# Half of the tiles of a matmul round moved to an idle PSUM pool, and an uneven split of the last output tile, in a fused attention + SwiGLU kernel

## The chip, the cores and the metric

The kernel runs on one core of a Trainium2 chip. The metric is the device time of one execution in microseconds (us), each figure a median of several runs. Every profile shown is from one execution, with times counted from the start of its span. Every timed run compared here is fast (granted TensorE clock 0.99 to 1.00).

Words used below: TensorE does the matmuls, VectorE and ScalarE move results from PSUM (the matmuls' accumulator memory, eight banks) to SBUF (the working memory), GpSimd issues most loads. To evacuate a bank is to move its result out, so that the next tile can have it. A load's issue is the row of the engine that starts it; it lands when its data is there.

## The reference

Attention through 32 memory slots per head, then a SwiGLU block, cut to what matters (8 batches, 8 heads, 576 positions, width 512, hidden width 1536):

```
a    = softmax(phi, over positions)              # per batch and head
k_m  = a^T k ;  v_m = a^T v                      # 32 x 64 memories
x    = softmax(q k_m^T / 8) v_m                  # tokens x 512
out  = (silu(x w_gate) * (x w_val)) w_out
```

The kernel folds `v_m` into the weights: U = v_m w, per batch, for gate and value. A "U round" below is the group of matmuls that makes U for one batch and one third ("chunk", 512 columns) of the hidden width; U is then multiplied with the attention weights to give gate and value.

## The kernel before

Two PSUM pools share the eight banks: `ps` (six) serves everything except output tiles, `po` (two) serves output tiles and, at the start, warm-up matmuls.

```python
work = ctx.enter_context(tc.tile_pool(name="work", bufs=3))
ps = ctx.enter_context(tc.tile_pool(name="ps", bufs=6, space=bass.MemoryType.PSUM))
po = ctx.enter_context(tc.tile_pool(name="po", bufs=2, space=bass.MemoryType.PSUM))
```

A U round fills two tiles for the gate weights and two for the value weights, then ScalarE ("a") and VectorE ("v") evacuate them:

```python
def u_round(b, parts, evac):
    banks = []
    for which, c, halves in parts:
        ...
        p = [ps.tile([128, 2, HC], FP32, tag="b", ...) for g in range(NG)]
        ...                      # matmuls into p[g]: rhs=W[w, c][64 * g:64 * g + 64, h0:h1, i]
        for g in range(NG):
            ...
            banks.append((dst, src, rSs[b][:, g, 0] if b in scaled else None))
    for (t, p, r), e in zip(banks, evac):
        ...                      # "a": nc.scalar.activation, "v": nc.vector.tensor_scalar
```

A slot makes one gate tile (ScalarE applies SiLU) and then the value tile of the slot before (VectorE multiplies it with that gate). So at each U round one value is left over:

```python
def gv_slot(b, s):
    n = len(pend)
    gv_gate(b, s)                # 2 matmuls into a ps bank, SiLU on ScalarE
    flush_mul(n)                 # 2 matmuls into a ps bank, multiplication on VectorE
```

The stretch of batches 0 and 1, and the last output tile:

```python
run([u_half(1, (0, 1), 0, 1, "av")] + g0[4:8] + g1[4:5])
for c in range(1, NCH):
    s = 8 * c
    run([u_item(0, c)] + g1[s - 3:s] + g0[s:s + 5])
    run([u_item(1, c)] + g0[s + 5:s + 8] + g1[s:s + 5])
run(g1[-3:])
flush_mul()
backlog = out_list(0) + out_list(1)
...
def out_units_end(c, u):         # two halves of 256 columns, each 12 matmuls,
    ...                          # a copy on ScalarE and two stores (SyncE and ScalarE queues)
```

Loads on GpSimd's queue (queries of batches 2 and 3 share one buffer):

```python
load_q(2)
load_q(3)                        # before the stretch; waits until batch 2's queries are transposed
...
if b == 2:                       # after the scores of batch 2
    load_k(3); load_v(3); load_q(4); load_phi(4, nc.gpsimd)
```

The softmax here doesn't subtract the row's maximum and nothing guards it: scores larger than these inputs give would overflow.

Of the kernel before, what the change touches and what calls it, by code (L numbers as in the profile page):

```python
# [9 lines left out]
FP32 = mybir.dt.float32  # L10
# [4 lines left out]
def kernel(  # L15
# [23 lines left out]
    DM, DF = moe_w_gate.shape  # L39
# [3 lines left out]
    NJF = DF // 128  # L43
# [11 lines left out]
# [3 lines that stand above are left out]
# [3 lines left out]
    out_r = out.rearrange("(b p j) c -> b j p c", b=B, p=P, j=J)  # L61
# [53 lines left out]
    HC = CH // 2  # L115
# [14 lines left out]
    WO = {}  # L130
# [234 lines left out]

    scaled = set()

    def u_round(b, parts, evac):


        banks = []
        for which, c, halves in parts:
            w0, w1, h0, h1 = which[0], which[-1] + 1, halves[0], halves[-1] + 1
            n = (h1 - h0) * HC
            p = [
                ps.tile([128, 2, HC], FP32, tag="b", name=f"p_u{g}").rearrange("p a f -> p (a f)")
                for g in range(NG)
            ]
            for w in which:
                o = (w - w0) * n  # L380
                for i in range(NP):
                    for g in range(NG):
                        nc.tensor.matmul(  # L383
                            p[g][32 * i:32 * i + 32, o:o + n],
                            lhsT=kTs[b][64 * g:64 * g + 64, 2, 32 * i:32 * i + 32],
                            rhs=W[w, c][64 * g:64 * g + 64, h0:h1, i],
                            start=True,
                            stop=True,
                            tile_position=(64 * g, 32 * i),
                        )  # L390
            for g in range(NG):
                if (b, c, g) not in Us:
                    Us[b, c, g] = upool.tile([128, 2, 2, HC], BF16, tag=f"U{c}{g}", name="t_U")
                if len(which) == 1:
                    dst = Us[b, c, g][:, h0:h1, w0]
                else:
                    dst = Us[b, c, g][:, h0]
                src = p[g][:, 0:(w1 - w0) * n].rearrange("p (a f) -> p a f", f=HC)
                banks.append((dst, src, rSs[b][:, g, 0] if b in scaled else None))
        for (t, p, r), e in zip(banks, evac):  # L400
            if e == "a":
                if r is None:
                    nc.scalar.copy(out=t, in_=p)  # L403
                else:
                    nc.scalar.activation(out=t, in_=p, func=AF.Copy, scale=r)
            elif r is None:
                nc.vector.tensor_copy(out=t, in_=p)  # L407
            else:
                nc.vector.tensor_scalar(out=t, in0=p, scalar1=r, scalar2=None, op0=ALU.mult)
# [5 lines left out]
    def flush_mul(n=None):  # L415
        for _ in range(len(pend) if n is None else n):
            pend.pop(0)()
# [16 lines left out]
    def gv_gate(b, s):  # L434

        jf, r = s // 2, s % 2
        if b % 2 == 0 and r == 0:
            hts[b // 2, jf] = hpool.tile([128, 2 * S], BF16, tag=f"h{jf}", name="t_h")
        gate = gv_half(b, s, 0)
        sg = work.tile([128, HALF], BF16, tag="sg", bufs=8, name="t_sg")  # L440
        nc.scalar.activation(out=sg, in_=gate, func=AF.Silu)  # L441
        col = (b % 2) * S + r * HALF
        dst = hts[b // 2, jf][:, col:col + HALF]

        def mul():
            val = gv_half(b, s, 1)
            nc.vector.tensor_tensor(out=dst, in0=sg, in1=val, op=ALU.mult)  # L447

        pend.append(mul)
# [14 lines left out]
    def token_segments(t0, count):  # L464
        segs = []
        t = t0
        while t < t0 + count:
            bb, rest = divmod(t, S)
            blk, pp = divmod(rest, P)
            n = min(P - pp, t0 + count - t)  # L470
            segs.append((t - t0, n, bb, 2 * (blk % 3) + blk // 3, pp))
            t += n
        return segs
# [30 lines left out]

    def out_units_end(c, u):

        h = DM // 2
        mine = {}

        def unit(half, jf):  # L510
            def run():
                if jf == 0:
                    mine["p"] = po.tile([128, h], FP32, tag="o", name="p_oo")
                nc.tensor.matmul(  # L514
                    mine["p"],
                    lhsT=hts[c, jf][:, 128 * u:128 * (u + 1)],
                    rhs=WO[jf][:, h * half:h * (half + 1)],
                    start=(jf == 0),
                    stop=(jf == NJF - 1),
                )  # L520
                if jf == NJF - 1:
                    t_o = work.tile([128, h], FP32, tag="to", name="t_o")
                    nc.scalar.copy(out=t_o, in_=mine["p"])
                    segs = token_segments(2 * c * S + 128 * u, 128)
                    for n, (r0, m, bb, jj, pp) in enumerate(segs):
                        (nc.sync, nc.scalar)[n % 2].dma_start(
                            out=out_r[bb, jj, pp:pp + m, h * half:h * (half + 1)],
                            in_=t_o[r0:r0 + m, :],
                        )

            return run

        return [unit(half, jf) for half in range(2) for jf in range(NJF)]

    def out_list(b):
        tiles = range(0, 4) if b % 2 == 0 else range(4, 9)
        res = []
        for n, u in enumerate(tiles):
            if b + 1 == B and u == tiles[-1]:
                res += out_units_end(b // 2, u)  # L540
            else:
                res += out_units(b // 2, u, "v" if n % 4 != 3 else "a")
        return res
# [3 lines left out]
            lambda g=g, n=n: q_T(b, g, n, evac[2 * g + n]) for g in range(NG) for n in range(2)  # L547
        ]

    def u_item(b, c, evac="avav"):  # L550

        return lambda: u_round(b, (((0,), c, (0, 1)), ((1,), c, (0, 1))), evac)

    def u_half(b, which, c, half, evac):

        return lambda: u_round(b, ((which, c, (half,)),), evac)

    def u_three(b):

        u_round(b, (((0,), 0, (0, 1)), ((1,), 0, (0, 1)), ((0,), 1, (0, 1))), "avavav")  # L560
# [4 lines left out]
    def run(items):  # L565
        for x in items:
            x()
# [13 lines left out]
    def gv_slots(b):  # L581
        return [lambda s=s: gv_slot(b, s) for s in range(2 * NJF)]
# [78 lines left out]

    g0, g1 = gv_slots(0), gv_slots(1)
    run([u_half(0, (0,), 0, 0, "av"), u_half(1, (0,), 0, 0, "av")])
    warm(6)
    for s in range(4):
        gv_gate(0, s)
    run([u_half(0, (1,), 0, 0, "va"), u_half(1, (1,), 0, 0, "va")])
    for s in range(2):
        gv_gate(1, s)
    flush_mul(3)  # L670
    run([u_half(0, (0, 1), 0, 1, "va")])
    flush_mul(2)
    run(g1[2:4])
    run([u_half(1, (0, 1), 0, 1, "av")] + g0[4:8] + g1[4:5])
    for c in range(1, NCH):
        s = 8 * c
        run([u_item(0, c)] + g1[s - 3:s] + g0[s:s + 5])
        run([u_item(1, c)] + g0[s + 5:s + 8] + g1[s:s + 5])
    run(g1[-3:])
    flush_mul()  # L680
    backlog = out_list(0) + out_list(1)
# [7 lines left out]
    for b in range(2, B):  # L689
# [30 lines left out]
        g = gv_slots(b)  # L720
# [3 lines left out]
        if last:  # L724
            streams += [([u_item(b, 2)], 5, 6)]
# [55 lines left out]
```

## Time and profile before

| | before |
|---|---|
| median time | 249.45 us (249.39 to 249.80, 3 runs) |
| TensorE busy | 96% of the span |
| first U round starts / first output matmul starts | 26.99 / 56.88 us |
| period of one U round with eight slots | 4.88 us |
| last output tile's first matmul / end of the span | 241.11 / 247.6 us |

The lines themselves stand in the prediction. In every row of a timeline the first number is the start and the second the duration. A pair of matmuls has a row of 0.41 us but the next pair starts 0.245 us later, so rows overlap, and stalls are read from the starts.

### The profile page before, as it was taken

The numbers are of one execution on the slowest core, as the hardware profiler recorded it, in microseconds if no ns is written. First come the engines' busy times: TensorE is split into PE (matmuls) and PEld (weight loads), VectorE is DVE, ScalarE is ACT, GpSimd is POOL, SyncE is SP. The second block draws the span as 40 slices with busy tenths as digits, with TensorE's granted clock in tenths as the row PEclk, the third lists the DMA queues.
The fourth block names the chain that finished last, engine by engine and source line by source line (L and its number), as shares of the span: only waits on it lengthen the run. The fifth ranks groups of instructions, "written<-read, shape, count | busy, mean of one in ns | idle before, by whom it ended". The sixth has DMA issues, their size and how long they took to land.

```text
span 247.6 us, 6587 instructions
## 1 busy us (share of the span) xinstructions
PE 237.5 (96%) x2573; PEld 152.3 (61%) x2600; DVE 158.9 (64%) x337; ACT 165.2 (67%) x356; POOL 54.5 (22%) x85
## 2 busy tenths in 40 slices
PE   7999999999999999999999999999999999999993
PEld 7966666665544765467645666476546655467543
DVE  0046599994437788479846778478846877587420
ACT  2447888886077667966896577966896577676201
POOL 8423455000060004060405420090007000000000
PEclk9999999999999999999999999999999999999998
DMA  7999999999689976996996599289425311310143
GB/s 182 206 204 203 196 197 201 233 199 198 134 158 248 231 168 95 207 282 145 125 243 191 94 175 249 91 119 196 94 51 123 65 42 42 87 42 0 45 128 85
DMA packets 49167, 37.00 MB, mean 149 GB/s; under 512 B 15984, under 2 KB 43888, under 8 KB 49136
## 3 DMA queue, kind: packets, MB, share of 16 engines
q0 software_dynamic: 27632, 22.42, 57.0%
q1 hardware_dynamic: 20496, 13.37, 22.7%
q10 hardware_dynamic: 1008, 0.79, 1.2%
q8 instruction: 20, 0.33, 0.5%
q14 instruction: 11, 0.09, 0.1%
HBM read 42.47 MB, written 9.44 MB: 210 GB/s over the span
## 4 chain that ended last, share of the span: by engine, by line
PE 87%; DMA 8%; POOL 2%; issue 2%; ACT 0%; POOLq 0%
PE p_oo L483 36%; PE p_g L425 20%; PE p_v L425 19%; DMA t_kv<-in_v_dram 8%; PE p_u L383 6%; PE p_kv L183 2%; PE p_oo L514 1%; POOL t_q L93 1%; POOL t_kv L81 1%; PE p_g L351 1%; PE p_v L351 1%; PE p_g L331 1%; PE p_vT L290 0%; PE p_kv L203 0%; PE p_oo L588 0%
## 5 line engine op out<-in xcount | busy, mean ns | idle before, releaser
L483 PE MATMUL p_oo<-WO,t_h 128*128 128x512 bf16 x393 | 101.6, 379 | 3.0 <-issue 2.9
L441 ACT ACTIVATE t_sg<-p_g 128x288 bf16<-128x288 f32 x192 | 76.9, 413 | 31.6 <-PE p_g L425 24.2
L447 DVE TENSOR_TENSOR t_h<-t_sg,p_v 128x288 bf16<-128x288 bf16 x192 | 84.3, 453 | 18.9 <-PE p_v L425 14.8
L425 PEld LDWEIGHTS <-t_U 128*128 128x128 bf16 x768 | 74.3, 98 | 30.7 <-issue 2.3
L425 PE MATMUL p_g<-t_A,t_U 128*128 128x288 bf16 x384 | 77.5, 286 | 0.4
L425 PE MATMUL p_v<-t_A,t_U 128*128 128x288 bf16 x384 | 76.8, 286 | 0.0
L483 PEld LDWEIGHTS <-t_h 128*128 128x128 bf16 x420 | 39.6, 98 | 41.0 <-issue 6.0
L495 DVE COPY t_o<-p_oo 128x512 f32<-128x512 f32 x27 | 18.6, 690 | 31.4 <-PE p_oo L483 31.3
L407 DVE CAST t_U<-p_u 128x512 bf16<-128x512 f32 x42 | 26.7, 684 | 6.8 <-PE p_u L383 6.8
L403 ACT CAST t_U<-p_u 128x512 bf16<-128x512 f32 x30 | 15.8, 592 | 8.9 <-PE p_u L383 8.9
L493 ACT COPY t_o<-p_oo 128x512 f32<-128x512 f32 x8 | 4.7, 589 | 19.9 <-PE p_oo L483 10.6
L100 POOL DMA_DIRECT2D t_q<-in_q_dram x6 | 4.7, 782 | 59.3 <-DMA t_qT<-t_q 58.5
L588 PE MATMUL p_oo<-bones 128*128 128x128 bf16 x198 | 15.7, 244 | 1.5 <-DVE bones L603 1.5
L383 PE MATMUL p_u<-W,t_kT 64*32 64x512 bf16 (+1 forms) x416 | 15.7, 365 | 0.1
L153 ACT ACTIVATE t_ephi<-t_phi 96x768 bf16<-96x768 f32 x16 | 12.5, 843 | 4.1 <-DMA t_phi<-in_phi_dram 4.1
L588 PEld LDWEIGHTS <-bones 128*128 128x128 bf16 x198 | 13.9, 111 | 2.1 <-DVE bones L603 1.5
L166 POOL COPY t_mark<-t_A 1x1 bf16<-1x1 bf16 x4 | 0.7, 181 | 55.7 <-DVE t_A L360 55.7
L341 ACT ACTIVATE t_E<-p_g 128x288 bf16<-128x288 f32 x16 | 6.6, 412 | 8.5 <-PE p_v L331 7.9
L360 DVE TENSOR_TENSOR t_A<-t_E,t_lz 128x576 bf16<-128x576 bf16 x16 | 11.5, 750 | 0.5 <-ACT t_lz L355 0.5
L355 ACT ACTIVATE t_lz<-t_lz 128x576 f32<-128x576 f32 x16 | 10.9, 684 | 0.5
L170 POOL TENSOR_TENSOR t_es<-t_es,t_ephi 96x256 f32<-96x256 f32 x16 | 10.7, 669 | 1.3
L383 PEld LDWEIGHTS <-t_kT 64*32 64x32 bf16 x416 | 4.8, 89 | 8.8 <-issue 7.3
(58 smaller groups left out, 167.9 us busy)
## 6 DMA issues: line engine op xcount, KB each, us to landing
t_kv<-in_k_dram POOLq DMA_DIRECT2D x8, 576.0 KB, 9.3
t_kv<-in_v_dram POOLq DMA_DIRECT2D x8, 576.0 KB, 14.2
out_dram<-t_o SPq DMA_DIRECT2D x23, 192.0 KB, 2.5
t_phi<-in_phi_dram POOLq DMA_DIRECT2D x6, 576.0 KB, 15.3
t_q<-in_q_dram POOLq DMA_DIRECT2D x6, 576.0 KB, 7.4
out_dram<-t_o SPq DMA_DIRECT2D x24, 128.0 KB, 2.5
W<-in_moe_w_gate_dram POOLq DMA_DIRECT2D x6, 256.0 KB, 12.9
W<-in_moe_w_val_dram POOLq DMA_DIRECT2D x6, 256.0 KB, 11.9
```

The lines of the kernel that those rows point to most:

```text
L153: nc.scalar.activation(out=t[:, :, g].rearrange("p j i m -> p i j m"), in_=src[:, g], func=AF.Exp)
L355: nc.scalar.activation(out=lz, in_=lz, func=AF.Exp, scale=-1.0)
L360: nc.vector.tensor_tensor(out=a, in0=es.pop((b, g)), in1=lzs.pop((b, g)), op=ALU.mult)
L383: nc.tensor.matmul(p[g][32 * i:32 * i + 32, o:o + n], lhsT=kTs[b][64 * g:64 * g + 64, 2, 32 * i:32 * i + 32], rhs=W[w, c][64 * g:64 * g + ...
L403: nc.scalar.copy(out=t, in_=p)
L407: nc.vector.tensor_copy(out=t, in_=p)
L425: nc.tensor.matmul(p[:, 0:HALF], lhsT=Us[b, c, g][:, o // 2, which, 128 * (o % 2):128 * (o % 2 + 1)], rhs=atts[b, g][:, r], start=(g == 0) ...
L441: nc.scalar.activation(out=sg, in_=gate, func=AF.Silu)
L447: nc.vector.tensor_tensor(out=dst, in0=sg, in1=val, op=ALU.mult)
L483: nc.tensor.matmul(mine["p"], lhsT=hts[c, jf][:, 128 * u:128 * (u + 1)], rhs=WO[jf], start=(jf == 0), stop=(jf == NJF - 1),)
L495: nc.vector.tensor_copy(out=t_o, in_=mine["p"])
L588: nc.tensor.matmul(p[:, 0:128], lhsT=bones, rhs=bones, start=True, stop=True)
```

## The change

The intent: while batches 0 and 1 are worked on, the two banks of `po` lie idle, so half of a U round's tiles (its value weights; in chunk 0 the whole of three half rounds) go there, and TensorE no longer waits for banks. At the end, an uneven split makes the last copy and the last store smaller.

```diff
-    def u_round(b, parts, evac):
+    def u_round(b, parts, evac, spare=-1):
-        for which, c, halves in parts:
+        for n_part, (which, c, halves) in enumerate(parts):
+            pool, tag = (po, "o") if n_part == spare else (ps, "b")
             p = [
-                ps.tile([128, 2, HC], FP32, tag="b", ...)
+                pool.tile([128, 2, HC], FP32, tag=tag, ...)
...
     def out_units_end(c, u):
-        h = DM // 2
+        parts = ((0, 3 * DM // 4), (3 * DM // 4, DM))
...
-    run([u_half(0, (1,), 0, 0, "va"), u_half(1, (1,), 0, 0, "va")])
+    run([u_half(0, (1,), 0, 0, "va"), u_half(1, (1,), 0, 0, "va", 0)])
...      # likewise the other half rounds of chunk 0
-        run([u_item(0, c)] + g1[s - 3:s] + g0[s:s + 5])
-        run([u_item(1, c)] + g0[s + 5:s + 8] + g1[s:s + 5])
+        run([u_item(0, c, spare=1)] + g1[s - 3:s] + g0[s:s + 5])
+        run([u_item(1, c, spare=1)] + g0[s + 5:s + 8] + g1[s:s + 5])
```

More of the change, by code (lines that the diff above doesn't have):

```diff
@@ L375, in u_round @@
             p = [
-                ps.tile([128, 2, HC], FP32, tag="b", name=f"p_u{g}").rearrange("p a f -> p (a f)")
+                pool.tile([128, 2, HC], FP32, tag=tag, name=f"p_u{g}").rearrange(
+                    "p a f -> p (a f)"
+                )
                 for g in range(NG)
@@ L505, in out_units_end, with unit @@
     def out_units_end(c, u):
-        h = DM // 2
+        parts = ((0, 3 * DM // 4), (3 * DM // 4, DM))
         mine = {}
-        def unit(half, jf):
+        def unit(c0, c1, jf):
             def run():
                 if jf == 0:
-                    mine["p"] = po.tile([128, h], FP32, tag="o", name="p_oo")
+                    mine["p"] = po.tile([128, c1 - c0], FP32, tag="o", name="p_oo")
                 nc.tensor.matmul(
@@ L516, in run @@
                     lhsT=hts[c, jf][:, 128 * u:128 * (u + 1)],
-                    rhs=WO[jf][:, h * half:h * (half + 1)],
+                    rhs=WO[jf][:, c0:c1],
                     start=(jf == 0),
@@ L521, in run @@
                 if jf == NJF - 1:
-                    t_o = work.tile([128, h], FP32, tag="to", name="t_o")
+                    t_o = work.tile([128, c1 - c0], FP32, tag="to", name="t_o")
                     nc.scalar.copy(out=t_o, in_=mine["p"])
@@ L526, in run @@
                         (nc.sync, nc.scalar)[n % 2].dma_start(
-                            out=out_r[bb, jj, pp:pp + m, h * half:h * (half + 1)],
+                            out=out_r[bb, jj, pp:pp + m, c0:c1],
                             in_=t_o[r0:r0 + m, :],
@@ L531, in unit @@
             return run
-        return [unit(half, jf) for half in range(2) for jf in range(NJF)]
+        return [unit(c0, c1, jf) for c0, c1 in parts for jf in range(NJF)]
     def out_list(b):
@@ L548, in q_items, with u_item, u_half @@
         ]
-    def u_item(b, c, evac="avav"):
-        return lambda: u_round(b, (((0,), c, (0, 1)), ((1,), c, (0, 1))), evac)
-    def u_half(b, which, c, half, evac):
-        return lambda: u_round(b, ((which, c, (half,)),), evac)
+    def u_item(b, c, evac="avav", spare=-1):
+        return lambda: u_round(b, (((0,), c, (0, 1)), ((1,), c, (0, 1))), evac, spare)
+    def u_half(b, which, c, half, evac, spare=-1):
+        return lambda: u_round(b, ((which, c, (half,)),), evac, spare)
     def u_three(b):
@@ L670 @@
     flush_mul(3)
-    run([u_half(0, (0, 1), 0, 1, "va")])
+    run([u_half(0, (0, 1), 0, 1, "va", 0)])
     flush_mul(2)
     run(g1[2:4])
-    run([u_half(1, (0, 1), 0, 1, "av")] + g0[4:8] + g1[4:5])
+    run([u_half(1, (0, 1), 0, 1, "av", 0)] + g0[4:8] + g1[4:5])
     for c in range(1, NCH):
         s = 8 * c
-        run([u_item(0, c)] + g1[s - 3:s] + g0[s:s + 5])
-        run([u_item(1, c)] + g0[s + 5:s + 8] + g1[s:s + 5])
+        run([u_item(0, c, spare=1)] + g1[s - 3:s] + g0[s:s + 5])
+        run([u_item(1, c, spare=1)] + g0[s + 5:s + 8] + g1[s:s + 5])
     run(g1[-3:])
```

## The prediction

> **What bounds the kernel now.** I read the page first (engine totals, slices, chain of waits), then the timeline of the stretch that the change touches, 26 to 57 us, engine by engine, then the timeline of the last 8 us.
>
> ```profile
> PE 237.5 (96%) x2573; PEld 152.3 (61%) x2600; DVE 158.9 (64%) x337; ACT 165.2 (67%) x356; POOL 54.5 (22%) x85
> PE 87%; DMA 8%; POOL 2%; issue 2%; ACT 0%; POOLq 0%
> ```
>
> The engine totals and the chain say the same: TensorE is the bound from 25.8 us to the end; the DMA share is the wait for the values of batch 1 before that. VectorE and ScalarE appear as no limit over the whole span. But "busy" hides short stalls, because a matmul's row is longer than the distance to the next one. So I read starts, not busy shares. In the stretch that the change touches, one round for U and eight gate/value slots repeat every 4.88 us (U rounds start at 40.62, 45.50, 50.38). One such period, TensorE only:
>
> ```profile
> 45.50 0.63 PE L383 MATMUL p_u<-W,t_kT 64*32 64x512 bf16 x16
> 46.06 0.42 PE L425 MATMUL p_g<-t_A,t_U 128*128 128x288 bf16 x2
> 46.32 0.41 PE L425 MATMUL p_v<-t_A,t_U 128*128 128x288 bf16 x2
> 46.72 0.41 PE L425 MATMUL p_g<-t_A,t_U 128*128 128x288 bf16 x2
> 46.96 0.41 PE L425 MATMUL p_v<-t_A,t_U 128*128 128x288 bf16 x2
> 47.29 0.41 PE L425 MATMUL p_g<-t_A,t_U 128*128 128x288 bf16 x2
> 47.59 0.41 PE L425 MATMUL p_v<-t_A,t_U 128*128 128x288 bf16 x2
> 47.84 0.41 PE L425 MATMUL p_g<-t_A,t_U 128*128 128x288 bf16 x2
> ```
>
> The columns are start, duration, engine, line and what is done. Undisturbed, two matmuls of 288 columns start every 0.245 us (47.59 to 47.84). Here the third pair comes 0.40 after the second (0.155 late), the fifth 0.33 after the fourth (0.085 late), the sixth 0.30 later (0.055 late). These add to 0.30 us per period, and the rest of the period has none. The evacuations that they wait for:
>
> ```profile
> 45.98 0.69 ACT L405 ACTIVATE t_U<-p_u,t_rS 128x512 bf16<-128x512 f32 x1 [0.20 <-PE p_u L383]
> 46.56 0.68 ACT L405 ACTIVATE t_U<-p_u,t_rS 128x512 bf16<-128x512 f32 x1
> 46.05 0.75 DVE L409 TENSOR_SCALAR t_U<-p_u,t_rS 128x512 bf16<-128x512 f32 x1
> 46.71 0.74 DVE L409 TENSOR_SCALAR t_U<-p_u,t_rS 128x512 bf16<-128x512 f32 x1
> 47.37 0.45 DVE L447 TENSOR_TENSOR t_h<-t_sg,p_v 128x288 bf16<-128x288 bf16 x1
> ```
>
> The pool has six banks and hands them out in turn. A U round takes four, the first gate and value the other two, and the next four tiles take over the four U banks. ScalarE's two evacuations end at 46.67 and 47.24, and the late gate pairs start 0.05 after each (46.72, 47.29). VectorE's second ends at 47.45 and the late value pair starts 0.14 later (47.59). So the waits are for banks, and I take 0.05 and 0.14 us as the delays from an end on ScalarE and VectorE to TensorE.
>
> **What the Trainium skill says.** "PSUM — Partial Sum Buffer", section "Specifications (TRN2)": 8 banks of 2 KiB. So the pools of six and two use all there is; the trace shows the pool of two used only by the 128x128 warm-up matmuls before the first output tile at 56.88. "Perfetto Trace Analysis", section "Optimization Strategy", says that a consistent bubble on the engine that should be saturated can mean too few buffers; the repeating late starts above are that. "TensorE: Matmul & The Clock Gate", section "Back-to-back issue gap", has N/2.4 + 2.5 ns for an isolated matmul, and says that loading weights makes it about 81 ns at N=128. The trace has 109.6 ns at 256 columns with changing weights (242.20 to 242.31 for one), which fits the first; for 128 columns it has the 24 warm-up matmuls in 1.51 us with a tail of 0.22, so 56 ns, though with the same weights reloaded. "Perfetto Trace Analysis", section "DMA Instruction — HWDGE (DVE, Sync)", says that the issuing sequencer is free for the next instruction only at the end of its DMA row. The trace agrees on ScalarE at the start (the issue at 0.74 takes 0.43, the table load begins at 1.2).
>
> **Part one: two of a U round's four tiles in the other pool.** No instruction is added or removed, the order on every engine stays (the comparison of instructions shows only line numbers moved). Per period U now holds two of the six banks and both of the other two; those two were last evacuated a period ago, so they never block. Then, from the start T of a U round:
> - Undisturbed starts on TensorE: gate 0 at 0.56, the leftover value at 0.81, gate 1 at 1.05, value 0 at 1.30, gate 2 at 1.54, value 1 at 1.79, gate 3 at 2.03, value 2 at 2.28.
> - In turn over six banks, gate 2 and value 1 take the two U banks: free at 1.22 and 1.44. No wait left. All three stalls of today go.
> - But value 2 now gets the bank of the leftover value (as today). VectorE multiplies that one only after both its U evacuations, from T+1.87 (47.37 - 45.50) for 0.45, plus 0.14: 2.46. Against 2.28 to 2.29 undisturbed that is a new wait of 0.17.
>
> So 0.30 becomes 0.17: 0.13 us per period, for the three periods from 40.62: 0.39 us. VectorE doesn't take over as the long-run bound: with work queued, its multiplications start 0.363 apart (47.37, 47.73) and its U evacuations 0.66 apart, 8 x 0.363 + 2 x 0.66 = 4.22 per period against 0.56 + 8 x 0.49 = 4.48 on TensorE.
>
> The first such period, from 35.75, is different:
>
> ```profile
> 35.75 0.89 PE L383 MATMUL p_u<-W,t_kT 64*32 64x512 bf16 x16
> 36.57 0.42 PE L425 MATMUL p_g<-t_A,t_U 128*128 128x288 bf16 x2
> 33.80 0.74 DVE L409 TENSOR_SCALAR t_U<-p_u,t_rS 128x512 bf16<-128x512 f32 x1
> 34.46 1.92 DVE L447 TENSOR_TENSOR t_h<-t_sg,p_v 128x288 bf16<-128x288 bf16 x5
> 36.30 0.74 DVE L409 TENSOR_SCALAR t_U<-p_u,t_rS 128x512 bf16<-128x512 f32 x1
> ```
>
> Here the gate follows U after 0.82 instead of 0.56: the second half of U itself waits for banks (0.26). With the other pool it does not. VectorE though is back to back from 30.58 to here (1.92 for five is 0.367 apart), so it reaches the leftover value no sooner than 36.30 + 2 x 0.66 = 37.62, and value 2 starts no sooner than 37.62 + 0.45 + 0.14 = 38.21. Today it starts at 38.49: 0.28 us won. The small rounds before (27 to 35.7 us) give nothing: their few stalls end where ScalarE has gone through its queue (the value matmuls at 30.07 follow its U evacuation, which ends at 30.02), or are swallowed by the full VectorE. Sum of part one: 0.28 + 0.39 = 0.67 us. It goes to the end one for one, as TensorE is on the chain from there on and later reads are long in place (the transposed queries of batch 2 land near 66 for scores at 69.8).
>
> **Part two: the last tile at 384 + 128 columns instead of 256 + 256.** The present tail:
>
> ```profile
> 241.11 2.78 PE L514 MATMUL p_oo<-WO,t_h 128*128 128x256 bf16 x24
> 242.62 0.37 ACT L523 COPY t_o<-p_oo 128x256 f32<-128x256 f32 x1 [0.72 <-PE p_oo L514]
> 243.02 0.37 ACTq L526 DMA_DIRECT2D out_dram<-t_o  x1
> 243.93 0.37 ACT L523 COPY t_o<-p_oo 128x256 f32<-128x256 f32 x1 [0.94 <-PE p_oo L514]
> 244.33 0.38 ACTq L526 DMA_DIRECT2D out_dram<-t_o  x1
> ```
>
> TensorE: 12 x 0.1625 = 1.95 (estimate from 384/2.4 + 2.5 ns) and 12 x 0.056 = 0.67, together 2.62 as against 24 x 0.1096 = 2.63: nothing. The last copy: 589 ns at 512 columns and 370 at 256 make 0.26 at 128, so 0.11 less. But the first copy is now 0.48 long and late: matmuls to 243.06, copy from 243.26 to 243.74, its store issued on ScalarE's queue from 243.77 to 244.15. The second part is ready at 243.06 + 0.67 + 0.20 = 243.93, and ScalarE is still issuing. So its copy starts about 244.15, ends at 244.41, and the last store is issued near 244.44, 0.11 later than today's 244.33. The stores land 1.7 to 2.3 us after issue, mostly fixed; half the bytes may give back a few hundredths. Part two: +0.1 us.
>
> **Rivals.** First, VectorE binds: the value tiles still share six banks, and the new wait of 0.17 grows to eat all of 0.30. For it speaks that VectorE is back to back up to 38 us; against, that from 48.11 its multiplications start 0.49 apart, paced by TensorE. Part one would give 0.28 at most, the time would be about 249.3. Second, the whole bubble vanishes because VectorE's row end is not what TensorE waits for: 4 periods, 0.28 + 3 x 0.30 = 1.2 us, and early rounds a little: 248.2 with the tail. Third, the tail works as intended, ScalarE issuing its store beside the copy: 0.67 + 0.11 + a little, 248.6. Fourth, a store or load that now meets other traffic: TensorE waits for no DMA after 26 us, so I give it little.
>
> **Range and chances.** 249.45 - 0.67 + 0.1 = 248.88, so 248.9. Rivals lie between 248.2 and 249.3, the three runs before differ by 0.4. I take 248.2 to 249.6. Two per cent is 5 us, more than all stalls of the stretch together, so "within 2%" is almost sure.
>
> **What would show it.** Periods of the U rounds of 4.75 instead of 4.88 us; the matmuls after a U round starting every 0.245 up to value 2 and that one late by 0.17, behind the multiplication of the leftover value; the second half of U at 36 us without its 0.26 wait; the first output matmul near 56.2 instead of 56.88. In the tail, the last copy on ScalarE starting right at the end of its own store issue, and the last issue some 0.1 us further from the last matmul's end than now. I'd be wrong if the periods stay at 4.88 or fall to 4.6, if the gain at 57 us is lost again by 241 us, or if the 128-column matmuls take 81 ns with changing weights (another 0.3 us on the tail).

## The result, and the profile after

The changed kernel took 249.24 us (248.98 to 249.40, 4 runs) against 249.42 us (249.38 to 249.80, 4 runs) for the kernel before: a ratio of 0.9988, 95% interval 0.9971 to 1.0006. Ratios here and below are the mean time of one kernel's fast runs over that of the other's of the same rounds, so not quite the ratio of the quoted medians. The prediction's 248.9 was 0.3 us low; its range holds the result. The interval holds 1, so these runs alone do not show a gain.

The page of the changed kernel, chain of waits:

```profile
PE 74%; DMA 20%; POOL 3%; issue 1%; ACT 0%; ACTq 0%; POOLq 0%
```

The busy shares tell nothing (TensorE 97% against 96%). The chain does: its DMA share went from 8% to 20%, so it now runs through loads on which it did not rest before. One period of the stretch, TensorE and the first instructions after the U evacuations on VectorE and ScalarE:

```profile
45.35 0.63 PE L386 MATMUL p_u<-W,t_kT 64*32 64x512 bf16 x16
45.91 0.42 PE L428 MATMUL p_g<-t_A,t_U 128*128 128x288 bf16 x2
46.17 0.41 PE L428 MATMUL p_v<-t_A,t_U 128*128 128x288 bf16 x2
46.41 0.41 PE L428 MATMUL p_g<-t_A,t_U 128*128 128x288 bf16 x2
46.66 0.41 PE L428 MATMUL p_v<-t_A,t_U 128*128 128x288 bf16 x2
46.90 0.41 PE L428 MATMUL p_g<-t_A,t_U 128*128 128x288 bf16 x2
47.15 0.41 PE L428 MATMUL p_v<-t_A,t_U 128*128 128x288 bf16 x2
47.44 0.41 PE L428 MATMUL p_g<-t_A,t_U 128*128 128x288 bf16 x2
47.74 0.41 PE L428 MATMUL p_v<-t_A,t_U 128*128 128x288 bf16 x2
```
```profile
47.22 0.45 DVE L450 TENSOR_TENSOR t_h<-t_sg,p_v 128x288 bf16<-128x288 bf16 x1
```
```profile
46.98 0.41 ACT L444 ACTIVATE t_sg<-p_g 128x288 bf16<-128x288 f32 x1
```

The old stalls are gone: the six pairs from 45.91 to 47.15 start 0.24 to 0.26 apart. Two short ones are left: gate 3 starts 0.29 after its predecessor, 0.05 after the SiLU of gate 0 ends (46.98 + 0.41 = 47.39), and value 2 starts 0.30 later, 0.07 after the multiplication of the leftover value ends (47.67). Together they make value 2 start 0.11 us late, and the period is 4.69 us (U rounds start at 40.66, 45.35 and 50.04) instead of 4.88.

The first period of the second chunk and the key/value sums of batch 3, the two places where a load now holds TensorE, and, on GpSimd, the first and third of the three loads issued one after the other from 68.50, of which the third is the one waited for:

```profile
35.58 0.41 PE L386 MATMUL p_u<-W,t_kT 64*32 64x512 bf16 x8
36.30 0.41 PE L386 MATMUL p_u<-W,t_kT 64*32 64x512 bf16 x8 [0.31 <-DMA W<-in_moe_w_val_dram]
```
```profile
85.84 0.35 PE L183 MATMUL p_kv<-t_kv,t_ephi 96*32 96x128 bf16 x12 [0.22 <-DMA t_kv<-in_v_dram]
```
```profile
68.50 0.77 POOL L100 DMA_DIRECT2D t_q<-in_q_dram  x1 [25.36 <-DMA t_qT<-t_q]
```
```profile
70.03 0.77 POOL L85 DMA_DIRECT2D t_kv<-in_v_dram  x1
```

The second half of the U round at 35.58 starts 0.72 after the first, where 0.23 is undisturbed: it waits for the value weights of chunk 1. At 85.84 TensorE waits for the values of batch 3, issued at 70.03 behind two other loads, which had waited for the transposed queries. In the kernel before, the views mark no wait for a DMA at either place. The landings say more. The value weights of chunk 1 land at 36.09 in the kernel before and at 36.16 in the changed one, and the second half of U starts at 36.23 and 36.30, 0.14 later in both: TensorE waited for them before the change too, but its earlier rows last to 36.16, so almost none of the wait is idle time. The values of batch 3 land at 85.45 before (the sums start at 86.08) and at 85.80 after (85.84).

The tail:

```profile
243.02 0.48 ACT L527 COPY t_o<-p_oo 128x384 f32<-128x384 f32 x1 [1.36 <-PE p_oo L518]
243.53 0.38 ACTq L530 DMA_DIRECT2D out_dram<-t_o  x1
244.16 0.27 ACT L527 COPY t_o<-p_oo 128x128 f32<-128x128 f32 x1 [0.66 <-DMA out_dram<-t_o]
244.46 0.38 ACTq L530 DMA_DIRECT2D out_dram<-t_o  x1
```

The last copy starts at 244.16, 0.25 after the end of ScalarE's own store issue (243.91). The last store is issued 3.59 us after this tile's first matmul (240.87), where it was 3.22.

The table counts from fixed points of each trace, so that a shift at the start does not enter:

| profiled run of | first U round | from it to the first output matmul | from there to the last tile | last tile to the end of the span |
|---|---|---|---|---|
| before | 26.99 | 29.89 | 184.2 | 6.5 |
| changed | 26.96 | 29.39 | 184.5 | 6.7 |

So this run gained 0.50 us in the U rounds, lost 0.3 at the wait for the values of batch 3 and 0.2 in the tail. Both profiled runs have the same span, 247.6 us, and the same granted clock, 0.996.

### The profile page after: what moved, and what is told of

It is laid out like the page before. It is cut to its first block, busy times and chain, and to the rows that moved or that the text cites. A ratio compares the mean times of both kernels' runs of the same rounds, so it can differ in the third digit from the quotient of the medians.

```text
span 247.6 us, 6614 instructions
## 1 busy us (share of the span) xinstructions
PE 240.1 (97%) x2600; PEld 151.4 (61%) x2600; DVE 158.5 (64%) x337; ACT 165.1 (67%) x356; POOL 54.5 (22%) x85
## 4 chain that ended last, share of the span: by engine, by line
PE 74%; DMA 20%; POOL 3%; issue 1%; ACT 0%; ACTq 0%; POOLq 0%
PE p_oo L486 31%; PE p_g L428 17%; PE p_v L428 17%; DMA t_kv<-in_v_dram 14%; PE p_u L386 4%; DMA W<-in_moe_w_val_dram 4%; DMA t_qT<-t_q 2%; PE p_kv L183 2%; POOL t_q L93 1%; POOL t_kv L81 1%; PE p_oo L518 1%; PE p_g L351 0%; PE p_v L351 0%; PE p_g L331 0%; POOL t_q L100 0%
## 5 line engine op out<-in xcount | busy, mean ns | idle before, releaser
L486 PE MATMUL p_oo<-WO,t_h 128*128 128x512 bf16 x420 | 108.6, 379 | 0.0
L444 ACT ACTIVATE t_sg<-p_g 128x288 bf16<-128x288 f32 x192 | 76.6, 413 | 31.3 <-PE p_g L428 24.2
```

What stands on the lines that cost most here:

```text
L444: nc.scalar.activation(out=sg, in_=gate, func=AF.Silu)
L486: nc.tensor.matmul(mine["p"], lhsT=hts[c, jf][:, 128 * u:128 * (u + 1)], rhs=WO[jf], start=(jf == 0), stop=(jf == NJF - 1),)
```

## The experiments

The theory: moving banks takes 0.5 us or more from the stretch; loads with a pace of their own (the weights of chunk 1, the values of batch 3) take some of it back; the new tail costs 0.1 to 0.3 us. The rivals: the gain is chance; the new tail helps; other waits in the stretch (VectorE's queue) take the gain.

The first four ran on one chip with 11 runs of the kernel before (median 249.47).

**The changed kernel again** (no edit).

> The changed kernel once more, unaltered, in five rounds. Theory (gain in the U rounds of 0.5 us, of which about 0.3 is lost at the wait for the values of batch 3, and a tail that is 0.3 to 0.4 longer to the last issue but lands a little sooner): 0.1 to 0.3 us below before. Rival (the change does nothing, the first four runs were chance): 0.0 to 0.05. The first output matmul near 56.35 and the key/value sums of batch 3 waiting until about 85.8 in its trace, as in the first profile, whatever the total.

Measured: 249.20 us (249.11 to 249.80), ratio 0.9990, interval 0.9979 to 1.0002. Output began at 56.40, near the expected 56.35. But its trace shows no wait for the values of batch 3 (they landed at 84.97), so that part of the expectation failed: the wait is there in some runs only. A wait of 0.3 us for value weights was in this run in the round of chunk 0, at 31.3. The interval still touches 1, so this run alone does not show a gain.

**Banks only** (last tile at 256 + 256 as before).

> U rounds in the other pool, last tile at 256 + 256 as before. Theory: first output matmul near 56.35 (0.53 before the old one), wait for the values of batch 3 until about 85.8, the last half tile starts about 0.24 earlier than before, and the tail from there to the last store's issue is 3.22 us as before; total 0.2 to 0.3 us below before, and below the full change by about 0.1. Rival (the new tail is a gain): slower than the full change by 0.1.

Measured: 248.89 us (248.76 to 249.60), ratio 0.9979, interval 0.9967 to 0.9992. This is a clear gain of about 0.6 us (0.3 more than expected). It is about 0.3 less time than the full change on the same chip, but the two intervals overlap. The last issue comes 3.23 us after the last tile's first matmul. This trace too waits for the value weights of chunk 1 (0.35 us, at 36.18), but nothing is lost at the sums of batch 3: from the first output matmul to the last tile it is 184.2 us, as before.

**Tail only** (384 + 128, no banks moved).

> Only the last tile at 384 + 128 columns. Theory: from the first matmul of that tile to the last store's issue 3.59 us instead of 3.22, the last copy starting 0.25 after the end of ScalarE's own store issue because of three semaphore waits in its queue; stores of half the size land 0.1 to 0.3 sooner; total +0.05 to +0.25 over before. Rival (intent of the change): the shorter last copy and store win 0.1 to 0.2.

Measured: 249.66 us (249.48 to 249.70), ratio 1.0004, interval 0.9992 to 1.0016. The time alone doesn't tell. The trace does: the last issue comes at 3.59, and the span (unrounded) ends 6.73 us after the tile's first matmul instead of 6.53. The changed kernel and its repeat show 6.73 and 6.71, and all nine traces with 256 + 256 lie between 6.52 and 6.56. So the new split costs about 0.2 us at the end; the intended gain isn't there.

**Banks, and the keys and values of batch 3 issued early.**

```diff
     load_q(2)
+    load_k(3)
+    load_v(3)
     load_q(3)
...
-            load_k(3)
-            load_v(3)
             load_q(4)
```

> U rounds in the other pool, old tail, and the keys and values of batch 3 issued ahead of the queries of batch 3 (whose buffer is free only after the transposing load of batch 2, and which therefore hold up GpSimd's queue until 68.5). Theory: no wait at the key/value sums of batch 3; the 0.5 us won by 57 us is still there at the last tile; total 0.45 to 0.6 below before, 0.25 to 0.3 below the banks alone. Rival (something else takes the gain between 57 us and the end, or the earlier loads disturb the weights): same total as the banks alone or worse.

Measured: 251.04 us (250.85 to 252.37), ratio 1.0069, interval 1.0051 to 1.0086. The expectation was wrong: the kernel got slower. The transposing load of batch 2 on SyncE, here first in the changed kernel and then in this one, and TensorE's wait in this one:

```profile
62.95 3.10 SPq L106 DMA_TRANSPOSE t_qT<-t_q  x1
```
```profile
63.06 5.59 SPq L106 DMA_TRANSPOSE t_qT<-t_q  x1
```
```profile
70.74 0.28 PE L331 MATMUL p_g<-t_qT,t_kT 64*32 64x288 bf16 x1 [1.50 <-DMA t_qT<-t_q]
```

The early loads were still under way when the transposing load began (issued at 44.51 and 47.11, they took 20.9 and 21.6 us to land); that took 5.59 us to issue instead of 3.10, landed near 70.7 instead of 67.9, and the scores of batch 2 waited 1.5 us. The rival "earlier loads disturb" holds, though it was the queries and not the weights. Three kernels were built on this version, so their totals are spoiled; their traces up to 57 us, and of the tail, are not.

**The kernel before, with weights that have landed (wrong result).** In the U round for batch 0 and chunk 1, the value half reads the gate weights of that chunk, which land earlier.

```diff
-    rhs=W[w, c][64 * g:64 * g + 64, h0:h1, i],
+    rhs=W[0 if (b, c) == (0, 1) else w, c][64 * g:64 * g + 64, h0:h1, i],
```

> Wrong result on purpose: the kernel before, with batch 0's second-chunk value round reading the first chunk's value weights, which have long landed. Theory (the 0.26 us in the middle of the U round at 35.75 is a wait for the weights to land, not for banks): the second half of that round starts 0.22 to 0.25 after the first instead of 0.45. Rival (banks, as predicted): still 0.4 or more.

(The text names the first chunk's value weights; the edit takes the gate weights of the same chunk.) Measured: one run at 249.59 us. In the trace:

```profile
35.91 0.71 PE L383 MATMUL p_u<-W,t_kT 64*32 64x512 bf16 x16
36.55 0.42 PE L425 MATMUL p_g<-t_A,t_U 128*128 128x288 bf16 x2
```

The gate follows the U round after 0.64 us instead of 0.82, so 0.18 of the 0.26 us that the prediction had put down to banks was the weights. Yet value 2 of that period starts 2.58 us after the U round, exactly as in the kernel before (35.75 to 38.33), and the next U round follows after 4.87 us in both. So the wait for weights hid bank waits of the same period: without it, gate 2 and value 1 start 0.34 and 0.30 after their predecessors (at 37.70 and 38.00), where it was 0.245 and 0.28.

**Banks and early keys, the same substitution (wrong result).**

> Wrong result on purpose: banks and early keys and values, and the same substitution of weights. Theory: in the U round near 35.6 the second half starts 0.22 to 0.25 after the first instead of 0.72, then TensorE runs until the value that waits for VectorE's queue; first output matmul 0.2 to 0.4 earlier than in the same kernel with the right weights, so near 56.0 to 56.15. Rival (VectorE's queue gives nothing back there): no change at 56.35.

Measured: the total of 251.54 us is spoiled. The second half of U follows at once, value 2 starts 2.39 us after the U round (35.55 to 37.94; 2.79 in the changed kernel), the period is 4.69 us, and the first output matmul starts at 55.92, 0.43 before that of the changed kernel. Against its true counterpart with early keys (56.18) it is 0.26, but 0.14 of that is an earlier start: from the first U round to the output the two take 28.99 and 29.11 us, so the substitution is worth 0.12 there, less than expected, and 0.40 against the changed kernel (29.39). So with the banks moved, the weights' landing is what TensorE waits for in that round, by an amount that differs from run to run.

**Two changes of order in the U rounds, on banks and early keys.** The evacuation of the two `po` tiles comes one slot later, and the first round of chunk 1 one slot later.

```diff
+    def u_late(b, c, slots):
+        late = []            # u_round leaves the evacuation of the po tiles here
+        first = lambda: u_round(
+            b, (((0,), c, (0, 1)), ((1,), c, (0, 1))), "avav", 1, late
+        )
+        return [first, slots[0], lambda: run(late)] + slots[1:]
...
-    run([u_half(1, (0, 1), 0, 1, "av", 0)] + g0[4:8] + g1[4:5])
+    run([u_half(1, (0, 1), 0, 1, "av", 0)] + g0[4:8] + g1[4:6])
-        run([u_item(0, c, spare=1)] + g1[s - 3:s] + g0[s:s + 5])
-        run([u_item(1, c, spare=1)] + g0[s + 5:s + 8] + g1[s:s + 5])
+        run(u_late(0, c, g1[s - 3 + (c == 1):s] + g0[s:s + 5]))
+        run(u_late(1, c, g0[s + 5:s + 8] + g1[s:s + 5]))
```

> Banks and early keys and values, and two changes of order: the evacuation of the two tiles in the other pool comes one gate/value slot later on both engines, and the first U round of the second chunk comes one slot later. Theory: the leftover value is multiplied before VectorE's second U evacuation, so no late starts are left after a U round and periods are 4.58 to 4.62 instead of 4.69; the weights have landed when the shifted round needs them; first output matmul near 55.7 to 56.0; total 0.3 to 0.6 below the banks with early keys and values. Rival (order only moves the waits): periods of 4.69 or more.

Measured: 251.19 us in total, spoiled as above (scores again wait 1.5 us), so the expected total was missed. The periods are as expected: U rounds at 40.52, 45.10 and 49.69, 4.58 and 4.59 us apart, and output begins at 55.89.

**The last copy on VectorE, on banks and early keys, 384 + 128.**

> Banks, early keys and values, the last tile at 384 + 128, but the last copy on VectorE, so that it does not stand behind ScalarE's store issue and its waits. Theory: the last copy starts about 2.85 us after the first matmul of that tile (3.29 in the changed kernel) and the last store is issued at about 3.15 (3.59, and 3.22 with 256 + 256); total 0.1 to 0.3 below the banks with early keys and values. Rival (the time at the end is the landing of the first part's stores or is fixed): no difference.

Measured: 251.25 us, against 251.04 for the same kernel with the old tail, on another chip: no difference that this could show. In the trace the last copy starts 2.82 us after the tile's first matmul, as expected, but the span ends 6.68 after it, where 256 + 256 has 6.52 to 6.56. The gain at the copy and at its issue (3.14 us) is there and does not reach the end.

The next three ran on one chip, with a median of 249.59 us for the kernel before.

**Banks only, and batch 3's values ahead of its queries, held until the transposing load has landed.** A copy of one element that reads the transposed queries holds GpSimd's queue.

```diff
     load_q(2)
-    load_q(3)
...
+            mark = att.tile([1, 1], BF16, tag="mark", bufs=1, name="t_mark")
+            nc.gpsimd.tensor_copy(out=mark, in_=qTs[2, 0][0:1, 0, 0:1])
             load_k(3)
             load_v(3)
+            load_q(3)
             load_q(4)
```

> Banks, old tail, and on GpSimd's queue after the transposing load of batch 2 (a copy of one element of its result holds the queue until then) first the keys and values of batch 3, then the queries of batch 3. Theory (the wait at the key/value sums of batch 3 near 85.4 takes part of the gain, and only because the values are third in line at 70.0): values issued about 0.6 earlier and landed well before 85, no wait of TensorE for them, the last tile starts 0.1 to 0.3 earlier relative to the first U round than with the banks alone, total 0.0 to 0.3 below the banks alone (so ratio to before about 0.997). Rival (the transposing load is disturbed, as when the same loads were sent at 44 us): scores of batch 2 wait for the transposed queries, total above before.

Measured: 248.85 us (248.70 to 249.00), ratio 0.9971, interval 0.9959 to 0.9983. The values are issued at 69.14 instead of 70.03, no wait for them is left, and the transposing load is not disturbed. The intervals of this version and of the banks alone overlap, so what the order of loads is worth by itself isn't shown.

This trace tells something else. Its first U round starts late, at 27.29, as the values of batch 1 landed late. The views mark no wait for weights (the second half of U starts at 36.23, 0.13 after they landed and 0.10 late, which the period does not show), all its periods are 4.69 us, and from the first U round to the output it takes 28.99 us: 0.90 less than before. But as it began late, its first output matmul starts at 56.28. With the banks moved and the old order of rounds, seven traces (the changed kernel and its repeat, banks alone, banks with early keys, the tail on VectorE, this one and the next with more buffers) have it between 56.18 and 56.41, though their first U rounds start between 26.81 and 27.41. The two that begin after 27.2 (this one and the one with more buffers) take 28.99 and 29.00 us to the output, as the run with substituted weights does (28.99); the other five wait longer for value weights (the repeat for those of chunk 0) and take 29.11 to 29.52. In all fourteen traces the value weights of chunk 1 land between 35.97 and 36.23, whatever TensorE does, and where it waits for them it starts 0.13 to 0.14 after.

**The same with the two changes of order.**

> The same, and the two changes of order in the U rounds that gave periods of 4.58 us before (evacuation of the tiles in the other pool one slot later; first U round of the second chunk one slot later). Theory: first output matmul 0.8 to 1.0 us earlier than before relative to the first U round (0.5 with the banks alone), kept to the end; total 0.7 to 1.1 us below before, ratio 0.996 to 0.997. Rival (a load that comes at its own time takes it: the transposing load ends at 68 whatever TensorE does): a wait of the scores of batch 2 or of the sums of batch 3 for a DMA, and a total as with the banks alone.

Measured: 248.26 us (248.10 to 248.36), ratio 0.9946, interval 0.9934 to 0.9958: the fastest version of all, 1.3 us under the kernel before. TensorE's U rounds in the second chunk:

```profile
44.81 0.62 PE L386 MATMUL p_u<-W,t_kT 64*32 64x512 bf16 x16
...
49.39 0.63 PE L386 MATMUL p_u<-W,t_kT 64*32 64x512 bf16 x16
```

The distance is 4.58 us, and the trace has no wait of TensorE for a DMA after the first U round. Output begins at 55.59, 28.67 us after the first U round (1.22 less than before, where 0.8 to 1.0 was expected), and from there to the last tile it is 184.2 as before: all of it is kept.

**The full change, with two SBUF buffers of their own for the last two parts.**

```diff
-    t_o = work.tile([128, c1 - c0], FP32, tag="to", name="t_o")
+    t_o = work.tile([128, c1 - c0], FP32, tag="te", bufs=2, name="t_o")
```

> The full change, with two buffers of their own for the last tile's two parts in SBUF. Theory (the 0.25 us between the end of ScalarE's store issue and the last copy are waits for the buffers' earlier stores, long landed, read one by one in its queue): the last copy starts 0.02 to 0.06 after the end of the store issue instead of 0.25, the last store is issued 3.35 to 3.4 us after that tile's first matmul instead of 3.59; total 0.1 to 0.2 below the full change. Rival (the waits are for something else or the issue itself takes that long): still 3.55 or more.

Measured: 249.07 us (248.87 to 249.81), ratio 0.9984, interval 0.9970 to 0.9997.

```profile
243.30 0.38 ACTq L530 DMA_DIRECT2D out_dram<-t_o  x1
243.72 0.27 ACT L527 COPY t_o<-p_oo 128x128 f32<-128x128 f32 x1 [0.45 <-PE p_oo L518]
```

The copy now starts 0.04 after the end of the issue (243.68), and the last store is issued at 3.37. So the 0.25 us were the waits of the shared buffers for earlier stores, which are read one after the other in ScalarE's queue: three of them in the chain of waits of the changed kernel, at 243.95, 244.01 and 244.08. But the span still ends 6.66 us after the tile's first matmul, as in the full change. The last bytes move 4.81 us after it, as before the change (4.82; 4.97 in the changed kernel); what then takes longer stays open.

**The two changes of order without the held queue** (another chip; kernel before 249.43 there).

> Banks, old tail, the two changes of order in the U rounds, but GpSimd's queue as in the changed kernel (queries of batch 3 ahead of its keys and values). Theory (the values of batch 3 land at their own time, near 85.2 to 85.8, and TensorE now gets there near 84.6): TensorE waits 0.5 to 1.0 us for them at the key/value sums, the first output matmul is as early as with the held queue (55.6 to 55.9), and the total is 0.3 to 0.7 above that version, ratio to before 0.9965 to 0.998. Rival (the load follows TensorE and lands earlier too): no wait, ratio 0.9946.

Measured: 248.81 us (248.34 to 249.84), ratio 0.9974, interval 0.9955 to 0.9993. The total lies where the theory put it, but not for its reason: this trace has no wait for the values of batch 3. The waits for loads that it has in the stretch are for weights (0.2 and 0.4 us, the longer in the round of chunk 0 at 31.3 us), and the output begins at 56.11, where 55.6 to 55.9 was expected. How much of the difference to the version with the held queue comes from the queue, and how much from the chip and the landing of weights, isn't separated.

## Why the prediction was right or wrong

The range held, but an unchanged kernel (249.45) would have lain in it too, and neither set of runs of the full change shows the direction by itself: both intervals reach 1. The point, 248.9, was 0.3 us too low against both sets. Of the 0.67 us forecast for the stretch 0.50 came, and that this is close is in part luck: two terms were too small and one had the wrong sign.

- **All old stalls go, one new wait comes:** right. The gain per steady period was put at 0.13 and is 0.19 us (4.88 to 4.69), three times, 0.57 instead of 0.39. The mis-sized term is the new wait, put at 0.17: it measures 0.11. The delay after VectorE was taken as 0.14 from one place and is 0.07 at the place that counts. The start of the multiplication (1.87 us after the U round) and its length (0.45) were right. A second wait, of gate 3 for the SiLU of gate 0 (0.05), was not listed, but lies inside the 0.11. That another order of evacuations removes these waits with the same banks is shown by the reordered rounds with 4.58 us.
- **First period of chunk 1, +0.28:** this step failed. The changed kernel takes 5.08 us from that U round to the next, the kernel before 4.87. There were two errors. "Today it starts at 38.49" was read from the chain of waits, whose pieces start later than the matmuls: the timeline has 38.33, so by its own rule the term was 0.12. And the 0.26 us inside the U round was put down to banks without checking for a load; the substitution of weights showed 0.18 of it to be weights, and the landing at 36.09 stands 0.14 before the start. "TensorE waits for no DMA after 26 us" was thus already false of the kernel before, though no view marked the wait. Moving banks could not end it: the weights land near 36.1 whenever TensorE comes, and it came 0.17 earlier.
- **The small rounds give nothing:** wrong by 0.14 us. From the first U round to that of chunk 1, the kernel before takes 8.76 us, the changed one 8.62. With 0.57, minus 0.21 for the first period, this makes the 0.50 measured.
- **It goes to the end one for one:** true of the repeat, the banks alone and the later versions that keep the early keys out (184.2 us from the first output matmul to the last tile); false in the first profile, which lost 0.3 us to the values of batch 3. (The transposed queries of batch 2 land at 67.95, not near 66, where only the row of their issue ends; the scores at 69.76 did not wait.) The fourth rival (a load that is now in the way), given "little", is the one that came.
- **The tail, +0.1:** the mechanism was right to the hundredth as far as it went (copy at 2.15, store issue at 2.66, its end at 3.04 us after the first matmul), and the size was off. The last copy was to start at the end of the issue and started 0.25 later, because of semaphore waits that in the kernel before (243.44 to 243.60) lay hidden behind the wait for TensorE. The 128-column matmuls took 56 ns, so that sign of being wrong did not come. At the end of the span about 0.2 us are lost.
- **The rivals:** VectorE as a bound did not come true. The tail as intended did not either. A bubble that vanishes altogether needs the changed order of evacuations.

The banks alone, near 0.6 us in timed runs, give more than the net 0.2 to 0.3 of the whole change. The tail gives some of it back, and the weights' landing near 36.1 us caps the rest: of the traces with the banks moved and the old order, the earliest start (26.81) brings the output to 56.22 and the latest (27.41) to 56.41. That cap is read from landings in all traces and from one substitution; a run with earlier weights was not made.

## What to carry to other kernels

When a stall is removed ahead of a load that paces itself, look up when that load lands before counting the gain: a view that marks no wait can hide one (here a landing at 36.09 and the start of its user at 36.23). When a bank goes to the next user in turn, order the evacuations by who needs the bank first; here that was worth another 0.11 us of each steady period, after the 0.19 of the two extra banks. And check that the engine is free when a smaller last piece is ready: here a store issue and the buffer's semaphore waits on the same queue put the last issue 0.37 us later, though the last copy was 0.11 shorter; and freeing the engine did not bring the end forward to where it was.

## What the Trainium skill lacked or had wrong

- "TensorE: Matmul & The Clock Gate", "Back-to-back issue gap": gives about 81 ns at N=128 and 131 ns at N=512 for a stream with weight loads. Here the twelve 128-column matmuls of the last part, with new weights each, start 56 ns apart (242.88 and 242.93 among them), and those of 512 columns 216 ns; the formula for the isolated gap fits both.
- "Perfetto Trace Analysis", "Identifying Dependency Chains": says that extra semaphore instructions may be put ahead of an instruction, but this section gives no time for them. Here three of them, for stores that had landed by 242.26, made 0.25 us between the row end of ScalarE's store issue (243.91) and its next copy (244.16).
- "DMA: Bandwidth & Descriptors", "Rules for kernel authors": says that a transposing load next to ordinary ones needs nothing. That is about correct data; two loads of 576 KB under way beside it made its issue 5.59 instead of 3.10 us long and its landing 2.8 us later.
- No page was found that has the time from the end of an evacuation to the next matmul into its bank: here 0.05 us after ScalarE and 0.07 to 0.14 us after VectorE.
